# Linear attention and a mixture of experts on one core: the first layer's results in four one-bank tiles, routing's products moved to another bank, and another order of the first loads

## The chip, the core and the metric

The kernel runs on one core of a Trainium2 chip. A core has TensorE (PE, matrix products and transposes; its weight loads are shown as PEld), VectorE (DVE), ScalarE (ACT), GpSimd (POOL), SyncE (SP, which here issues most DMAs) and 16 DMA engines. Products land in PSUM, eight banks of 128 partitions x 512 fp32 values. The metric is the device time of one execution in microseconds.

## The reference

Two steps, all in fp32. First linear attention with positive random features on 8 batches x 8 heads x 576 positions x 64 values (128 features):

```python
def phi(x):                              # x = q or k, scaled by D ** -0.25
    h = einsum('bhsd,md->bhsm', x, omega) - sum(x * x) / 2
    return exp(h - max(h)) / sqrt(m)
kv  = einsum('bhsm,bhsd->bhmd', k_p, v)
z   = sum(k_p, axis=2)
out = einsum('bhsm,bhmd->bhsd', q_p, kv) / (einsum('bhsm,bhm->bhs', q_p, z) + 1e-06)
```

Its result, turned to 4608 rows of 512 values, goes through a mixture of 8 experts. `x @ w_gate` gives each row its expert (the largest logit) and a weight (that expert's softmax). The row's output is the weight times `relu(x @ w1[e]) @ w2[e]`, with w1 512 x 1024 and w2 1024 x 512.

## The kernel before, in words

The order of work on every engine is written out by hand: each engine runs its instructions in the order of the program text, and a framework adds the semaphore waits from what each tile's accesses need. A tile is taken from a pool under a tag; tiles of one tag share that tag's buffers.

**PSUM.** One pool holds all eight banks: tags `tr`, `t2`, `kf` and `nu` of one bank each, and `pp` with two buffers of two banks each.

**Attention** (line 57 on) works in 72 units: for each batch the remainder (head "-1", the last 64 positions of all heads), then its 8 heads. `run` (line 259) is a software pipeline. In iteration i TensorE does, in this order, for unit u = i: the projections (`unit_b1`, L139, into `pp`); for unit i+1 the transposes of k and q (`unit_a1`, L124, into `tr`); for unit i-1 the transposes of q's features (`unit_ct`, L194, into `t2`); for i-2 the gated key-value product (`unit_df`, L211, into `kf`); for i-1 the key-value product (`unit_ckv`, L179, into `kf`); for i-3 the numerators (`unit_dn`, L230, into `nu`). VectorE takes the maximum (L145), copies the transposes (L130) and scales the numerators (L244, L247, which read `nu`). ScalarE does the exponentials (L153) and copies (L187, L199, L217). POOL adds keys (L165 to L167).

**Routing** (line 331 on) puts each row in its expert's list. Its small steps stand in a queue, filled once per batch; `some(n)` runs the next n. It is called twice per iteration: behind `unit_cq`, and behind `unit_dn`. Four steps have TensorE products in a bank of their own tag `kf`: `s0` (L435, in odd batches), `s3` (L456 to L459), and `f0` (L529) and `f5` (L557) of a part that finds the first expert's rows ahead of time. That bank is also the key-value product's.

**Experts** (line 656 on). Rows are gathered in slots of 2 x 128 rows of one expert. `step` (line 844) does for slot t and for four groups g: 24 products of the first layer (`l1`, L788; fp32 as high and low parts, three products each) into bank `p_1[g]`; ScalarE's relu (L802) that reads it and gives the high part hh; VectorE's L806 that reads it and gives the low part hl. Then come the next slot's transposes (L769), and the second layer (`l2`, L813 to L815) into `p_2[0]` and `p_2[1]`, which take the tags `kf` and `nu`. At a change of expert the new weights are split into high and low parts on ScalarE (L51) and VectorE (L45).

The four banks `p_1` are made by `half`, two at a time:

```python
t = self.ps.tile([P, 2, 512], F32, name=f"p_1{len(self.p_1)}", tag="pp", bufs=2)
self.p_1 += [t[:, i, :] for i in range(2)]
```

**The drain of attention.** After the last unit, `run` finishes the last units between the first slot's transposes (`rows`, L697) and the first products of an early slot 0 (`products0`, L714, in plain fp32). The last two units' numerators go to the two banks of one more `pp` tile, `nu_last`; the last remainder's go to `t2`.

**The loads.** `load(b)` (line 93) issues on SP the remainders of k, q and v (`kqr`, and `rv` for v, L105), then k, q and v for two heads at a time (L108). `rv` waits for POOL to clear its tile (L90). The gate weights, which go into tile `G` (L85; L211 reads it), are issued in the constructor, ahead of the first load.

Of the kernel before, what the change touches and what calls it, by code (L numbers as in the profile page):

```python
# [8 lines left out]
F32 = mybir.dt.float32  # L9
# [9 lines left out]
P = 128  # L19
# [4 lines left out]
SM = 512  # L24
# [32 lines left out]
class Attention:  # L57
    def __init__(self, tc, ctx, ps, io, q, k, v, omega, wg, xs, routing, ident):
        self.tc, self.nc = tc, tc.nc
        self.q, self.k, self.v, self.xs, self.routing, self.ident = q, k, v, xs, routing, ident  # L60
        nc = tc.nc
        pool = lambda n, b, **kw: ctx.enter_context(tc.tile_pool(name=n, bufs=b, **kw))
        self.cp = pool("at_c", 1)
        self.io, self.ps = io, ps
        self.wk = pool("at_wk", 2)
        self.xo = pool("at_x", 2)
        cp = self.cp

        om = self.wk.tile([P, 2, D], F32, name="om", tag="kp")
        for i in range(2):  # L70
            nc.sync.dma_start(om[:, i, :], omega)
        pt = self.ps.tile([P, 512], F32, name="pt_om", tag="tr")
        nc.tensor.transpose(pt[:, :P], om.rearrange("p a d -> p (a d)"), ident)
        self.om = cp.tile([P, M], F32, name="omt")
        nc.scalar.mul(self.om, pt[:, :P], SCALE)

        self.G = cp.tile([P, H, W - 1], F32, name="G")
        self.one = cp.tile([P, 1], F32, name="one")
        nc.gpsimd.memset(self.one, 1.0)
        for a in range(2):  # L80
            r = slice(a * D, (a + 1) * D)
            for h in range(H):
                nc.gpsimd.tensor_copy(self.G[r, h, :D], ident[r, r])
            with nc.allow_non_contiguous_dma(reason="gate weights"):
                nc.sync.dma_start(self.G[r, :, D:], wg.rearrange("(h d) e -> d h e", d=D))  # L85


        self.rv = [[cp.tile([P, NP, D], F32, name=f"rv{i}{a}") for a in range(2)] for i in range(2)]
        for t in self.rv[0] + self.rv[1]:
            nc.gpsimd.memset(t, 0.0)  # L90
        self.st, self.last = {}, {}

    def load(self, b):
        nc, io = self.nc, self.io
        s = {}
        s["kqr"] = io.tile([P, 2, NP, D], F32, name=f"kqr_{b}", tag="kqr")
        for nm in "kq":
            s[nm] = io.tile([P, H, NJ, D], F32, name=f"{nm}_{b}", tag=nm)
        s["v"] = io.tile([P, H, NJ, D], F32, name=f"v_{b}", tag="v")
        s["vr"] = self.rv[b % 2]  # L100
        for n, src in enumerate((self.k, self.q, self.v)):
            rem = src[b, :, SM:, :].rearrange("(i a) p d -> a p i d", a=2)
            for a in range(2):
                to = s["vr"][a] if n == 2 else s["kqr"][:, n]
                nc.sync.dma_start(to[a * SR:(a + 1) * SR], rem[a])  # L105
        for c in range(0, H, 2):
            for to, src in ((s["k"], self.k), (s["q"], self.q), (s["v"], self.v)):
                nc.sync.dma_start(to[:, c:c + 2],  # L108
                                  src[b, c:c + 2, :SM, :].rearrange("h (p j) d -> p h j d", j=NJ))
        s["kva"] = self.xo.tile([P, H, W], F32, name=f"kva_{b}", tag="kva")  # L110
        s["x"] = self.xo.tile([P, NJ, H, D], F32, name=f"x_{b}", tag="x")
        s["xr"] = self.xo.tile([P, NP, D], F32, name=f"xr_{b}", tag="xr")
        s["lg"] = self.xo.tile([P, NJ, E, H], F32, name=f"lg_{b}", tag="lg")
        s["lgr"] = self.xo.tile([P, E, NP], F32, name=f"lgr_{b}", tag="lgr")
        self.st[b] = s
# [16 lines left out]
    def unit_b1(self, b, h):  # L132

        nc, s = self.nc, self.st[b]
        t, o = s[("th", h)], self.ps.tile([P, 2, 4, M], F32, name=f"pp_{b}_{h}", tag="pp", bufs=2)
        for n in range(4):
            for a in range(2):
                r = slice(a * D, (a + 1) * D)
                nc.tensor.matmul(o[:, a, n, :], t[r, n, :], self.om[r], start=True, stop=True)  # L139
        s[("pp", h)] = o  # L140
# [78 lines left out]
    def unit_dn(self, b, h):  # L219
        nc, s = self.nc, self.st[b]  # L220
        qt, kva = s[("qt", h)], s["kva"]
        pn = self.last.get((b, h))
        if pn is None:
            pn = self.ps.tile([P, 512], F32, name=f"nu_{b}_{h}", tag="nu")
        o = pn[:, :NJ * W].rearrange("p (j w) -> p j w", w=W)

        for j in range(NJ):
            for a in range(2):
                r = slice(a * SR, (a + 1) * SR)
                nc.tensor.matmul(o[r, j, :], qt[:, j, r], kva[:, h if h >= 0 else 2 * j + a, :], start=True, stop=True)  # L230
        de = self.wk.tile([P, NJ, 1], F32, name=f"de_{b}_{h}", tag="de")
        nc.vector.tensor_scalar_add(de, o[:, :, W - 1:W], EPS)
        s[("nu", h)] = o, de
# [25 lines left out]
    def run(self, pre):  # L259
        units = [(b, h) for b in range(B) for h in [-1] + list(range(H))]  # L260
        n = len(units)
        g = lambda i: units[i] if 0 <= i < n else None
        self.load(0)
        self.unit_a1(*units[0])
        self.unit_a2(*units[0])
        for i in range(n):
            u1, u, c, d, e = g(i + 1), g(i), g(i - 1), g(i - 2), g(i - 3)
            if u[1] == 0 and u[0] + 1 < B:
                self.load(u[0] + 1)
            pre.ahead(i - n)  # L270
            self.unit_b1(*u)
            self.unit_max(*u)
            self.unit_exp(*u, 0)
            if u1: self.unit_a1(*u1)
            else: pre.rows(0)
            if u1: self.unit_a2(*u1)
            self.unit_exp(*u, 1)
            if c: self.unit_ct(*c)
            if c: self.unit_cq(*c)
            self.routing.some(1)  # L280
            self.bank(i)
            if d: self.unit_df(*d)
            if c: self.unit_ckv(*c)
            if d: self.unit_dk(*d)
            if c: self.unit_ckt(*c)
            o = e if e and e[1] >= 0 else (e[0] - 1, -1) if e and e[0] > 0 else None
            if o: self.unit_dn(*o)
            if o: self.unit_rc(*o)
            self.routing.some(2 if i >= n - 6 else 1)
            if o: self.unit_out(*o)  # L290
            self.unit_sum(*u)
        c, d, e = g(n - 1), g(n - 2), g(n - 3)
        self.routing.some(1000)
        self.bank(n)
        two = self.ps.tile([P, 2, 512], F32, name="nu_last", tag="pp", bufs=2)
        self.last = {d: two[:, 0, :], c: two[:, 1, :]}
        self.unit_df(*d)
        self.unit_dk(*d)
        self.unit_dn(*e)
        self.unit_rc(*e)  # L300
        self.unit_out(*e)
        self.unit_ct(*c)
        self.unit_cq(*c)
        pre.rows(1)
        self.unit_ckv(*c)
        self.unit_ckt(*c)
        self.unit_dn(*d)
        self.unit_rc(*d)
        self.unit_out(*d)
        self.unit_df(*c)  # L310
        self.unit_dk(*c)
        pre.banks()
        pre.fill(1)
        self.last[(B - 1, -1)] = self.ps.tile([P, 512], F32, name="nu_rest", tag="t2")
        for o in (c, (B - 1, -1)):
            self.unit_dn(*o)
            self.unit_rc(*o)
            self.unit_out(*o)
# [11 lines left out]

class Routing:


    def __init__(self, tc, ctx, xs, ident):
        self.tc, self.nc, self.xs = tc, tc.nc, xs
# [76 lines left out]
        self.lr[o] = lr  # L412
        self.queue += self.group(b, g, slice(o * NJ, (o + 1) * NJ + o), [self.lr[0], self.lr[1]] if o else None)

    def some(self, n):
        for f in self.queue[:n]:
            f()
        self.queue = self.queue[n:]

    def group(self, b, g, sl, lr):  # L420
        nc, wk = self.nc, self.wk
# [234 lines left out]
class Experts:  # L656
# [40 lines left out]
        self.nc.scalar.copy(self.x0[:, :, a * P:(a + 1) * P], p.rearrange("p (c t) -> p c t", t=P))  # L697

    def banks(self):
        self.p_1 = []  # L700
        self.todo = [m for f in range(self.NF) for m in self.products0(f)]

    def half(self):

        t = self.ps.tile([P, 2, 512], F32, name=f"p_1{len(self.p_1)}", tag="pp", bufs=2)
        self.p_1 += [t[:, i, :] for i in range(2)]

    def products0(self, f):

        def product(c):  # L710
            if c == f % 4 == 0:
                self.half()
            o = self.p_1[f // 2][:, f % 2 * self.T2:(f % 2 + 1) * self.T2]
            self.nc.tensor.matmul(o, self.w1s[:, c, f * P:(f + 1) * P], self.x0[:, c, :],  # L714
                                  start=c == 0, stop=c == self.NC - 1)
# [192 lines left out]
def attention_moe(tc, q, k, v, omega, wg, w1, w2, out, xs):  # L908
    nc = tc.nc
    with ExitStack() as ctx:  # L910
# [7 lines left out]
        with ExitStack() as c2:  # L918
            io = c2.enter_context(tc.tile_pool(name="at_io", bufs=2))
            at = Attention(tc, c2, ps, io, q, k, v, omega, wg, xs, rt, ident)  # L920
            rt.open(ps, "kf")
            with sched():
                at.run(ex)
                ex.rest()
# [26 lines left out]
```

## Time and profile before

| | |
|---|---|
| median of 3 runs | 886.38 us (884.7 to 887.65) |
| the profiled execution | 891.42 us, its span 889.6 us |
| PE busy | 770.4 us (87%) |
| PEld busy | 672.9 us (76%) |
| DVE busy | 364.4 us (41%) |
| ACT busy | 342.6 us (39%) |
| POOL busy | 208.4 us (23%) |
| HBM | 61.10 MB read, 19.55 MB written |

The start takes up to about 16 us of the span, attention with its routing up to about 312 us, the drain and the early slot up to 360 us, the experts the rest. A row of the timeline reads: start in us, length in us, engine, line, operation, out<-in, shape, count, and in brackets how long the engine had been idle before it and what ended that. A row of waits reads: engine, line, what it waited for, us in total, times, longest. Busy times of TensorE are modelled at their ends, so a busy TensorE can still have room.

### The profile page before, as it was taken

The numbers are of one execution on the slowest core, as the hardware profiler recorded it, in microseconds if no ns is written. First come the engines' busy times: TensorE is split into PE (matmuls) and PEld (weight loads), VectorE is DVE, ScalarE is ACT, GpSimd is POOL, SyncE is SP. The second block draws the span as 40 slices with busy tenths as digits, with TensorE's granted clock in tenths as the row PEclk, the third lists the DMA queues.
The fourth block names the chain that finished last, engine by engine and source line by source line (L and its number), as shares of the span: only waits on it lengthen the run. The fifth ranks groups of instructions, "written<-read, shape, count | busy, mean of one in ns | idle before, by whom it ended". The sixth has DMA issues, their size and how long they took to land.

```text
span 889.6 us, 18594 instructions
## 1 busy us (share of the span) xinstructions
PE 770.4 (87%) x7147; PEld 672.9 (76%) x7147; DVE 364.4 (41%) x903; ACT 342.6 (39%) x1016; POOL 208.4 (23%) x364
## 2 busy tenths in 40 slices
PE   5998899988888889889898889888979887989883
PEld 3887788877777776778787778777868776878773
DVE  3677787877867758301111141110151124111110
ACT  2776766766656644311111241111151133111210
POOL 4432433323233311211101120111120111110110
PEclk9999999999989999999999989999989998999997
DMA  5661634606381111521001152101142116100000
GB/s 170 168 202 24 194 87 131 215 5 211 94 300 39 56 56 54 183 97 49 25 29 37 48 166 76 44 30 48 49 141 80 37 48 220 49 29 22 13 25 16
DMA packets 68459, 79.37 MB, mean 89 GB/s; under 512 B 27390, under 2 KB 51966, under 8 KB 68352
## 3 DMA queue, kind: packets, MB, share of 16 engines
q1 hardware_dynamic: 61792, 58.98, 21.1%
q0 software_dynamic: 6560, 19.03, 6.4%
q8 instruction: 59, 0.97, 0.5%
q14 instruction: 48, 0.39, 0.1%
HBM read 61.10 MB, written 19.55 MB: 91 GB/s over the span
## 4 chain that ended last, share of the span: by engine, by line
issue 47%; PE 19%; DVE 10%; DMA 9%; ACT 7%; POOL 5%; POOLq 1%; SPq 0%; DVEq 0%; ACTq 0%
DMA out_dram<-ys,idx 9%; PE pp L139 5%; DVE mx L145 4%; PE kf L179 3%; ACT kp L153 3%; PE nu L230 2%; PE t L194 2%; ACT qp L153 2%; PE tr L124 2%; PE kf L211 2%; POOL xgm L762 1%; POOL xg L762 1%; DVE rt_RH L506 1%; POOL out_dram L821 1%; DVE th L130 1%
## 5 line engine op out<-in xcount | busy, mean ns | idle before, releaser
L788 PE MATMUL p<-xh,w1p 128*128 128x256 f32 x1216 | 177.9, 289 | 65.2 <-DVE hl L806 64.9
L788 PEld LDWEIGHTS p<-xh,w1p 128*128 128x128 f32 x1216 | 160.3, 194 | 75.8 <-DVE hl L806 72.7
L806 DVE SCALAR_TENSOR_TENSOR hl<-p,hh 128x512 fp32r<-128x512 f32 x76 | 52.6, 692 | 387.3 <-ACT hh L802 383.5
L821 POOL DMA_INDIRECT out_dram<-ys,idx x38 | 39.0, 1026 | 430.7 <-ACT ys L820 323.4
L802 ACT ACTIVATE hh<-p 128x512 fp32r<-128x512 f32 x76 | 45.4, 598 | 229.8 <-PE p L788 227.0
L813 PE MATMUL p<-w2p,hh 128*128 128x512 f32 x288 | 115.2, 400 | 0.1
L815 PE MATMUL p<-w2p,hl 128*128 128x512 f32 x288 | 113.6, 394 | 0.0
L814 PE MATMUL p<-w2p,hh 128*128 128x512 f32 x288 | 113.5, 394 | 0.0
L153 ACT ACTIVATE kp<-pp,mx 128x128 f32<-128x128 f32 x256 | 73.2, 368 | 87.7 <-DVE mx L145 87.0
L788 PE MATMUL p<-xl,w1p 128*128 128x256 f32 x608 | 98.2, 284 | 0.0
L820 ACT ACTIVATE ys<-p,gt 128x512 f32<-128x512 f32 x38 | 26.2, 689 | 175.4 <-PE p L815 86.0
L165 POOL TENSOR_TENSOR k<-kp 128x256 f32<-128x256 f32 x64 | 46.5, 726 | 189.5 <-ACT kp L153 140.4
L145 DVE TENSOR_REDUCE mx<-pp 128x8 f32<-128x1024 f32 x64 | 78.1, 1220 | 16.4 <-PE pp L139 11.3
L788 PEld LDWEIGHTS p<-xl,w1p 128*128 128x128 f32 x608 | 84.4, 192 | 0.0
L139 PE MATMUL pp<-omt,th 64*128 64x128 f32 x1024 | 79.1, 297 | 2.1 <-DVE th L130 1.9
L153 ACT ACTIVATE qp<-pp,mx 128x128 f32<-128x128 f32 x256 | 74.3, 398 | 0.0
L139 PEld LDWEIGHTS pp<-omt,th 64*128 64x128 f32 x1024 | 66.4, 198 | 9.8 <-DVE th L130 3.3
L815 PEld LDWEIGHTS p<-w2p,hl 128*128 128x128 f32 x288 | 53.9, 187 | 13.4
L813 PEld LDWEIGHTS p<-w2p,hh 128*128 128x128 f32 x288 | 53.9, 187 | 12.7 <-issue 0.3
L814 PEld LDWEIGHTS p<-w2p,hh 128*128 128x128 f32 x288 | 54.0, 187 | 12.4
L230 PE MATMUL nu<-kva,qt 128*64 128x73 f32 x992 | 55.4, 238 | 0.0
L194 PE MATMUL t<-ident,qp 128*128 128x128 f32 x256 | 42.7, 292 | 4.4 <-ACT qt L199 1.2
(362 smaller groups left out, 1063.1 us busy)
## 6 DMA issues: line engine op xcount, KB each, us to landing
w1s<-in_moe_w_dram SPq DMA_DIRECT2D x5, 2048.0 KB, 9.4
w2s<-in_moe_w_dram SPq DMA_DIRECT2D x5, 2048.0 KB, 10.6
k<-in_k_dram SPq DMA_DIRECT2D x32, 256.0 KB, 5.3
q<-in_q_dram SPq DMA_DIRECT2D x32, 256.0 KB, 5.5
v<-in_v_dram SPq DMA_DIRECT2D x32, 256.0 KB, 5.7
token_rows<-x SPq DMA_DIRECT2D x8, 1024.0 KB, 7.9
kqr<-in_k_dram SPq DMA_DIRECT2D x16, 64.0 KB, 2.9
kqr<-in_q_dram SPq DMA_DIRECT2D x16, 64.0 KB, 2.5
```

What stands on the lines that cost most here:

```text
L139: nc.tensor.matmul(o[:, a, n, :], t[r, n, :], self.om[r], start=True, stop=True)
L145: self.nc.vector.tensor_reduce(out=mx, in_=s[("pp", h)], axis=AX.X, op=ALU.max, negate=True)
L153: self.nc.scalar.activation(o[:, j, :], p[:, a, 2 * n + i, :], AF.Exp, bias=mx[:, a, 2 * n + i:2 * n + i + 1])
L165: nc.gpsimd.tensor_tensor(out=k2, in0=kp[:, :2, :], in1=kp[:, 2:, :], op=ALU.add)
L194: nc.tensor.transpose(pt[:, j * P:(j + 1) * P], qp[:, j, :], self.ident)
L230: nc.tensor.matmul(o[r, j, :], qt[:, j, r], kva[:, h if h >= 0 else 2 * j + a, :], start=True, stop=True)
L788: return [lambda w=w, x=x, c=c, n=n: self.nc.tensor.matmul(o, w[:, c, f], x[:, c, :], start=n == 0, stop=n == len(ops) - 1) for n, (w, x, ...
L806: self.nc.vector.scalar_tensor_tensor(out=b, in0=self.p_1[g], scalar=0.0, in1=a.bitcast(F32), op0=ALU.max, op1=ALU.subtract)
L813: nc.tensor.matmul(p, h[:, c, k], self.w2h[:, c, :], start=c == 0, stop=False)
L814: nc.tensor.matmul(p, h[:, c, k], self.w2l[:, c, :], start=False, stop=False)
L815: nc.tensor.matmul(p, l[:, c, k], self.w2h[:, c, :], start=False, stop=c == self.NF - 1)
L821: self.nc.gpsimd.indirect_dma_start(out=self.out[:, :], in_=y, in_offset=None, bounds_check=NT - 1, out_offset=bass.IndirectOffsetOnAxis(a ...
```

## The change

1. `pp` leaves the common pool: attention has a pool `ps_a` of its own for it (two buffers of two banks). In the drain, behind the last `unit_cq`, that pool is closed, and a pool `ps_m` is opened with four tiles of one bank. `p_1[g]` is tile g of it. The last two units' numerators use tiles 2 and 3 before.
2. Routing's products use tag `nu` instead of `kf`. The first `some` of an iteration stands behind the copy of the transposes, ahead of q's exponentials; the second never runs a step that has products (`PRODUCTS`, by name) and stops ahead of one.
3. The first batch's loads: the remainders of k and q, then k and q of head 0, of head 1, v of both, then v's remainder, then the other heads as before. The gate weights come behind the whole first load. For later batches the order of the loads is as it was.
4. The numerators' products of a unit run their two halves in the order (1, 0).

```diff
@@ Attention.__init__
+        self.open = ExitStack()
+        self.pp = self.open.enter_context(tc.tile_pool(name="ps_a", bufs=2, space=PSUM))
...
-            with nc.allow_non_contiguous_dma(reason="gate weights"):
-                nc.sync.dma_start(self.G[r, :, D:], wg.rearrange("(h d) e -> d h e", d=D))
+        self.wg = wg
@@ Attention.load
-        for n, src in enumerate((self.k, self.q, self.v)):
-            rem = src[b, :, SM:, :].rearrange("(i a) p d -> a p i d", a=2)
-            for a in range(2):
-                to = s["vr"][a] if n == 2 else s["kqr"][:, n]
-                nc.sync.dma_start(to[a * SR:(a + 1) * SR], rem[a])
-        for c in range(0, H, 2):
-            for to, src in ((s["k"], self.k), (s["q"], self.q), (s["v"], self.v)):
-                nc.sync.dma_start(to[:, c:c + 2],
-                                  src[b, c:c + 2, :SM, :].rearrange("h (p j) d -> p h j d", j=NJ))
+        def rest(nms):
+            for n, src in nms:
+                rem = src[b, :, SM:, :].rearrange("(i a) p d -> a p i d", a=2)
+                for a in range(2):
+                    to = s["vr"][a] if n == 2 else s["kqr"][:, n]
+                    nc.sync.dma_start(to[a * SR:(a + 1) * SR], rem[a])
+
+        def main(nms, h):
+            for nm, src in nms:
+                nc.sync.dma_start(s[nm][:, h], src[b, h, :SM, :].rearrange("h (p j) d -> p h j d", j=NJ))
+
+        kq, v = (("k", self.k), ("q", self.q)), (("v", self.v),)
+        rest(((0, self.k), (1, self.q)))
+        if b == 0:
+            main(kq, slice(0, 1))
+            main(kq, slice(1, 2))
+            main(v, slice(0, 2))
+        rest(((2, self.v),))
+        for c in range(2 if b == 0 else 0, H, 2):
+            main(kq + v, slice(c, c + 2))
@@ Attention.unit_b1
-        t, o = s[("th", h)], self.ps.tile([P, 2, 4, M], F32, name=f"pp_{b}_{h}", tag="pp", bufs=2)
+        t, o = s[("th", h)], self.pp.tile([P, 2, 4, M], F32, name=f"pp_{b}_{h}", tag="pp")
@@ Attention.unit_dn
-            for a in range(2):
+            for a in (1, 0):
@@ Attention.run
         self.load(0)
+        for a in range(2):
+            with self.nc.allow_non_contiguous_dma(reason="gate weights"):
+                self.nc.sync.dma_start(self.G[a * D:(a + 1) * D, :, D:], self.wg.rearrange("(h d) e -> d h e", d=D))
...
             if u1: self.unit_a2(*u1)
+            self.routing.some(1)
             self.unit_exp(*u, 1)
             if c: self.unit_ct(*c)
             if c: self.unit_cq(*c)
-            self.routing.some(1)
...
-            self.routing.some(2 if i >= n - 6 else 1)
+            self.routing.some(2 if i >= n - 6 else 1, False)
...
-        two = self.ps.tile([P, 2, 512], F32, name="nu_last", tag="pp", bufs=2)
-        self.last = {d: two[:, 0, :], c: two[:, 1, :]}
...
         self.unit_cq(*c)
+        self.open.close()
+        pre.banks()
+        self.last = {d: pre.bank(2), c: pre.bank(3)}
         pre.rows(1)
...
-        pre.banks()
         pre.fill(1)
@@ Routing
+    PRODUCTS = ("s0", "s3", "f0", "f5")
...
-    def some(self, n):
-        for f in self.queue[:n]:
-            f()
-        self.queue = self.queue[n:]
+    def some(self, n, products=True):
+        while n and self.queue and (products or self.queue[0].__name__ not in self.PRODUCTS):
+            self.queue.pop(0)()
+            n -= 1
@@ Experts
     def banks(self):
+        self.pm = self.ctx.enter_context(self.tc.tile_pool(name="ps_m", bufs=1, space=PSUM))
...
-    def half(self):
-        t = self.ps.tile([P, 2, 512], F32, name=f"p_1{len(self.p_1)}", tag="pp", bufs=2)
-        self.p_1 += [t[:, i, :] for i in range(2)]
+    def bank(self, g):
+        return self.pm.tile([P, 512], F32, name=f"p_1{g}", tag=f"p_1{g}")
...
-            if c == f % 4 == 0:
-                self.half()
+            if c == f % 2 == 0:
+                self.p_1.append(self.bank(f // 2))
@@ attention_moe
-            rt.open(ps, "kf")
+            rt.open(ps, "nu")
```

## The prediction

> **What bounds the kernel now.** I read the page first, then the busy times by stage, then TensorE's waits, then the order of time at the places that those waits name.
>
> ```profile
> span 889.6 us, 18594 instructions
> ```
> ```profile
> 50.00:312.00 262.00, 237.09 (x3476) 207.35 (x3474) 199.85 (x573) 176.66 (x657) 91.13 (x164) 0.95 0.43 132
> ...
> 360.00:870.00 510.00, 444.64 (x2808) 397.05 (x2807) 107.94 (x168) 116.19 (x203) 85.33 (x111) 0.98 0.19 64
> ```
>
> The columns of the stage rows are length, PE, PEld, DVE, ACT, POOL, granted clock, DMA share, GB/s. TensorE is the engine that is full: 237 of 262 us in attention, 445 of 510 in the experts, where VectorE and ScalarE are busy a fifth of the time. What matters is why TensorE stops, and where its clock is halved. In the experts its idle time has one name, L806, the hidden layer's low part:
>
> ```profile
> PEld p L788 <- DVE hl L806: 72.7, 38, 4.8
> PE p L788 <- DVE hl L806: 64.9, 38, 4.6
> ```
> ```profile
> 390.04 0.60 ACT L802 ACTIVATE hh<-p 128x512 fp32r<-128x512 f32 x1 [2.06 <-PE p L788]
> 390.67 0.69 DVE L806 SCALAR_TENSOR_TENSOR hl<-p,hh 128x512 fp32r<-128x512 f32 x1 [13.08 <-ACT hh L802]
> ...
> 391.41 1.21 PE L788 MATMUL p<-xh,w1p 128*128 128x256 f32 x8 [1.47 <-DVE hl L806]
> ...
> 394.23 1.01 PEld L788 LDWEIGHTS p<-xh,w1p 128*128 128x128 f32 x8
> ...
> 398.74 1.01 PEld L788 LDWEIGHTS p<-xh,w1p 128*128 128x128 f32 x8 [1.62 <-DVE hl L806]
> ```
>
> A step has four groups g of 24 products. Group 1 starts at 391.41, after waiting for group 0's L806; group 2 at 394.23 without a wait; group 3 at 398.74, after waiting for group 2's. L806 reads p_1[g], the next group writes p_1[g+1]. Only 0-1 and 2-3 wait, and these are the pairs that share one two-bank tile. The wait follows the tile, not the bank. Two other places agree:
>
> ```profile
> 324.96 0.41 DVE L247 TENSOR_TENSOR x<-nu_last,de 128x256 f32<-128x256 f32 x1
> ...
> 325.52 0.73 PE L230 MATMUL nu_last<-kva,qt 128*64 128x73 f32 x16 [0.19 <-DVE x L247]
> ```
> ```profile
> 381.61 0.69 ACT L820 ACTIVATE ys<-p,gt 128x512 f32<-128x512 f32 x1 [4.97 <-PE p L815]
> ...
> 381.82 0.39 PE L815 MATMUL p<-w2p,hl 128*128 128x512 f32 x1
> ...
> 386.72 0.40 PE L815 MATMUL p<-w2p,hl 128*128 128x512 f32 x1
> ```
>
> nu_last is the other two-bank tile: products into its second bank wait for a read of its first. p_2's banks are one-bank tiles, and L815 runs on in one while L820 reads the other.
>
> **The change part by part.**
>
> *Four one-bank tiles for p_1.* Each group then writes a tile whose readers ran a step earlier. A group without a wait takes 394.23 less 391.41 = 2.82 us; from group 2 to group 3 it is 398.74 less 394.23 = 4.51, so a usual wait costs 1.69, and three long ones more. The weight-load row sums them to 72.7; I take 73, between the matmul row's 65 (whose ends are modelled) and 75. Late next is nothing: the second layer needs group 3's L806 only in its 21st product, and 21 products take 386.72 less 381.82 = 4.9 us, while L802 and L806 take 0.60 + 0.69.
>
> *The clock in the experts.* The three long waits (4.3 us and more) come at a change of expert, where L802 stands behind eight casts of weights on ScalarE. The group behind such a wait runs at half clock:
>
> ```profile
> 522.34 4.26 ACT L51 CAST w2p<-w2s 128x512 fp32r<-128x512 f32 x8
> ```
> ```profile
> 528.56:533.84 5.28, 5.28 (x24) 5.28 (x25) 0.50 0.89 241
> 558.18:561.00 2.82, 2.82 (x24) 2.82 (x25) 1.00 0.59 183
> ```
>
> The same 24 products take 5.28 against 2.82, 2.5 us more. Three times that is 7, which I take. Below it lies 0 (the clock drops anyway), above it 510 x (1 - 0.98) = 10.
>
> *Routing's products in the nu bank, behind the transposes.* Now they use kf, behind the copy L187 or ahead of L211:
>
> ```profile
> PE rr L456 <- ACT kvt L187: 11.3, 5, 2.5
> PE kf L211 <- DVE m L463: 3.0, 2, 2.0
> PE h_cnt L529 <- ACT kvt L187: 1.9, 1, 1.9
> PE rf L435 <- ACT kvt L187: 1.9, 1, 1.9
> PE kf L211 <- DVE rt_L L436: 1.4, 2, 0.7
> ```
> ```profile
> 112.13 0.18 PE L456 MATMUL rr<-rt_OH,rt_tri 128*128 128x40 bf16 x1 [2.10 <-ACT kvt L187]
> ...
> 112.35 1.16 PE L139 MATMUL pp<-omt,th 64*128 64x128 f32 x16
> ```
>
> Together 19.5 us (us in total, times, longest). At 112.13 the next unit's projection, L139, is queued behind the waiting product, so the whole unit slips. In the new order the product stands behind L139 and the transposes (1.16 us and more after the numerators), and nu's last reader, L247, belongs to the unit before; kf is left alone. The new wait is that of the next numerators for routing's read of nu, with the unit's transposes and key-value products between: I allow 0.1 to 0.2 us for each of 12 groups of products, 2 in all. The products' own time stays; a routing step comes half a unit later at most, and what uses the result (the gather of the first rows) stands whole units behind. So 17.5, from 8 (half the waits come back) to 19.5.
>
> Behind these stalls too the clock is halved; the first and the last of seven such stretches:
>
> ```profile
> 70.90:74.20 3.30, 3.30 (x28) 2.74 (x28) 2.22 (x5) 0.63 (x3) 0.00 (x0) 0.54 0.00 0
> ...
> 303.00:306.30 3.30, 3.30 (x38) 3.08 (x34) 1.27 (x8) 1.62 (x7) 1.36 (x3) 0.54 0.02 5
> ```
>
> Attention's 0.95 over 262 us is 13 us of full speed lost. I take 10 of it back, from 0 to 13. [...] The trace speaks for 10: each halved stretch stands behind a routing stall.
>
> *The halves of the numerators, (1, 0).* With the remainder's key-value product ahead, and without it (a unit behind a remainder):
>
> ```profile
> 93.26 0.27 PE L179 MATMUL kf<-kp_-1_1424,rv 128*64 128x128 f32 x1
> ...
> 94.08 1.16 PE L139 MATMUL pp<-omt,th 64*128 64x128 f32 x16
> ```
> ```profile
> 241.75 0.71 PE L230 MATMUL nu<-kva,qt 128*64 128x73 f32 x16
> ...
> 242.52 1.16 PE L139 MATMUL pp<-omt,th 64*128 64x128 f32 x16
> ```
>
> 0.82 against 0.77: that product, which fills the first half, costs 0.05 now. If the second half's numerators run beside it, up to 64 x 0.05 = 3 is won; if not, 0. I take 1.
>
> *k and q first.* Rows of the start:
>
> ```profile
> 1.75 1.42 SPq L85 DMA_DIRECT2D G<-in_moe_w_gate_dram  x2
> ...
> 3.21 1.29 SPq L105 DMA_DIRECT2D kqr<-in_k_dram  x2
> ...
> 9.03 1.29 SPq L105 DMA_DIRECT2D rv<-in_v_dram  x2
> ...
> 10.37 0.60 SPq L108 DMA_DIRECT2D k<-in_k_dram  x1
> ...
> 11.31 1.23 DVE L145 TENSOR_REDUCE mx_-1_228<-pp_-1_219 128x8 f32<-128x1024 f32 x1 [2.18 <-PE pp_-1_219 L139]
> ...
> 13.64 0.66 PE L124 MATMUL tr<-ident,k 128*128 128x128 f32 x2 [2.38 <-DMA k<-in_k_dram]
> ...
> 15.77 2.08 PE L139 MATMUL pp<-omt,th 64*128 64x128 f32 x16 [0.78 <-DVE th L130]
> ```
> ```profile
> 25.59 0.35 PE L211 MATMUL kf<-G,kvt 128*64 128x72 f32 x4
> ```
>
> SP's queue holds head 0's k behind rv, which waits until 9.03 for POOL to clear its tile. Without G ahead, kqr goes out at 1.75, 1.46 earlier, and so the first maximum starts at 9.85. Head 0's k goes out near 4.4 and lands 13.64 - 10.37 = 3.3 later, at 7.7, before TensorE is free of the first projection. Its transposes then end near 11.2, their copy waits for the maximum's end at 11.1, and L139 follows at 11.95 instead of 15.77: 3.8 gained. G goes out behind the nine remaining loads (up to 0.60 us each from 10.4, so near 15.8, and takes 1.42 to issue), and L211 would want it at 25.59 - 3.8 = 21.8. With 3.3 us to land it is there at 20.5; in a fuller queue it may be late, and then L211 and all behind it wait. I take 3.5, from 1 to 4.5. For later batches the order of the loads stays as it is.
>
> *The drain.* The new pool's tiles stand on the old pp slots, whose last readers are the exponentials of the last unit; TensorE has by then passed the transposes of their results. So nothing waits that did not wait, and nu_last's 0.19 goes: 0, from -1 to 1.
>
> Sum: 73 + 7 + 17.5 + 10 + 1 + 3.5 = 112. The profiled execution took 891.4 (span 889.6 and 1.8 around it) and would take 779; the median of the runs, 886.4, is 5.0 lower, which gives **774**.
>
> **The rivals.**
>
> *The wait stays.* The tiles of one pool might be watched together, or the wait have another owner. Then only 32 us come, and the median would be 854. [...] For it: the wait is there in spite of four banks. Against it: no wait between groups 1 and 2, none in p_2.
>
> *The long waits move.* At a change of expert the second layer waits for casts and L806 instead of the first. Three waits of 4.8 and their 7 us of slow clock come back, 21: 795. Against it: casts have the 11.3 us of four unbroken groups to finish.
>
> *Routing's stalls return in nu.* 27.5 are lost: 802 (774 + 27.5). For it: VectorE is busy 200 of 262 us there, and every unit's numerators use this one bank.
>
> *Slower.* TensorE without pauses is granted less clock, through attention and experts. After the change they last about 262 - 27.5 and 510 - 80, 665 us at full clock; a clock c adds 665 x (1/c - 1), and the 112 are eaten at c = 0.86. At 0.80 the time would be 774 + 166 = 940. Against it: the longest unbroken stretches, from one step's second layer into the next, show 1.00.
>
> **How the numbers follow.** The forecast's own case gets 0.79, the moved long waits 0.06, the returned routing stalls 0.05, the wait that stays 0.06, the slower clock 0.02, and 0.02 is left for no change. Low: all upper bounds, 75 + 10 + 19.5 + 13 + 3 + 4.5 + 1 = 126, so 760. High: the lower bounds 65 + 0 + 8 + 0 + 0 + 1 - 1 = 73 would give 813, but not all fall together; 797 holds the moved waits, and leaves out the last three cases and most of the routing one. Range 760 to 797. No change means within 0.3% (2.7 us), which is what the three runs spread. Faster 0.96, same 0.02, slower 0.02.
>
> **What would show it.** A step is now 418.22 less 391.41, 26.8 us:
>
> ```profile
> 418.22 1.21 PE L788 MATMUL p<-xh,w1p 128*128 128x256 f32 x8 [1.47 <-DVE hl L806]
> ```
>
> Right: L806 gone from TensorE's waits, a step of 23.4 us (26.8 less two waits), 1.00 in the experts; no L456 or L435 behind L187, and near 1.00 in attention; the second L139 near 12 us and L211 at 22 with no DMA ahead of it. Wrong: L788 still behind L806; L813 to L815 with a wait ahead of them; L230 behind L463 or L436; a granted clock below 1.00 in long stretches.

## Result and the profile after

| | before | after |
|---|---|---|
| median of 4 runs each | 886.09 us (884.7 to 887.65) | 778.29 us (777.73 to 778.81) |
| ratio | | 0.8783 (0.8767 to 0.8799) |
| the profiled execution, and its span | 891.42, 889.6 | 777.73, 775.9 |
| PE busy | 770.4 us (87%) | 740.8 us (95%) |

The kernel is 107.8 us faster by the medians, 113.7 by the two profiled executions. The prediction said 774, with a range of 760 to 797. Lines of the changed kernel are numbered higher: attention by 12 (L139 is L151, L187 is L199, L211 is L223, L230 is L242, L247 is L259), routing and the experts by 16 (L456 is L472, L788 is L804, L806 is L822, L815 is L831).

The busy times by stage of the changed kernel: attention, drain, experts.

```profile
span 775.9 us, 18503 instructions
```
```profile
50.00:285.00 235.00, 225.13 (x3449) 194.84 (x3447) 201.24 (x572) 174.55 (x653) 90.85 (x164) 1.00 0.46 144
285.00:332.00 47.00, 43.20 (x356) 31.33 (x355) 30.02 (x110) 20.11 (x51) 9.00 (x16) 1.00 0.27 88
332.00:760.00 428.00, 427.55 (x2805) 387.31 (x2804) 106.84 (x167) 114.81 (x201) 85.61 (x112) 1.00 0.22 77
```

The third column is TensorE's busy time. In the experts it is 427.55 of 428 us, and the granted clock is 1.00 in all three stages, from 50 to 760 us. TensorE's waits in the changed kernel, and the group of the first layer's products, whose last figure is the idle time ahead of it:

```profile
PE t L206 <- ACT qt L211: 4.6, 17, 0.4
...
PE kf L223 <- ACT kvt L199: 2.3, 1, 2.3
PE rr L472 <- DVE x L259: 1.5, 2, 0.8
...
PE nu L242 <- DVE h_v L547: 0.9, 1, 0.9
```
```profile
L804 PE MATMUL p<-xh,w1p 128*128 128x256 f32 x1216 | 167.8, 280 | 0.3
```

The 38 waits for the low part are gone (0.3 us of idle time is left), and so are routing's waits behind the copy L199. What remains behind the start is 1.1 us at most at a time, but for one wait of 2.3 us in the drain (L223 behind L199), which the kernel before had too. One kind of wait has grown: that of the transposes of q's features (L206) for ScalarE's copy of those before them. A step of the experts by the timeline, first products of two steps running:

```profile
376.56 1.10 PE L804 MATMUL p<-xh,w1p 128*128 128x256 f32 x8
...
399.95 1.10 PE L804 MATMUL p<-xh,w1p 128*128 128x256 f32 x8
```

It is 23.39 us, where it was 26.81. The start, in the same view:

```profile
1.76 1.40 SPq L107 DMA_DIRECT2D kqr<-in_k_dram  x2
...
4.51 0.60 SPq L111 DMA_DIRECT2D k<-in_k_dram  x1
...
10.08 1.23 DVE L157 TENSOR_REDUCE mx_-1_233<-pp_-1_224 128x8 f32<-128x1024 f32 x1 [2.18 <-PE pp_-1_224 L151]
...
11.96 2.08 PE L151 MATMUL pp<-omt,th 64*128 64x128 f32 x16 [0.88 <-DVE th L142]
...
22.56 0.35 PE L223 MATMUL kf<-G,kvt 128*64 128x72 f32 x4
```

Head 0's projection starts at 11.96 instead of 15.77 and waits for no DMA ahead of it. L223 starts at 22.56 without waiting for the gate weights.

Where the 113.7 us lie, between the same instructions in both profiled executions:

| stretch | before | after | difference | forecast |
|---|---|---|---|---|
| to the maximum of batch 1's remainder | 46.8 | 43.4 | -3.4 | -3.5 |
| from there to the maximum of the last head | 267.9 | 242.8 | -25.1 | -28.5 |
| from there to the first L788 (L804): the drain | 45.1 | 43.2 | -1.9 | 0 |
| from there to the end of the last L815 (L831) | 515.9 | 432.8 | -83.2 | -80 |

### The profile page after: what moved, and what is told of

Read it like the earlier page. It is cut to its first block, busy times and chain, and to the rows that moved or that the text cites. A ratio compares the mean times of both kernels' runs of the same rounds, so it can differ in the third digit from the quotient of the medians.

```text
span 775.9 us, 18503 instructions
## 1 busy us (share of the span) xinstructions
PE 740.8 (95%) x7147; PEld 650.9 (84%) x7147; DVE 366.7 (47%) x903; ACT 341.4 (44%) x1016; POOL 208.6 (27%) x364
## 5 line engine op out<-in xcount | busy, mean ns | idle before, releaser
L822 DVE SCALAR_TENSOR_TENSOR hl<-p,hh 128x512 fp32r<-128x512 f32 x76 | 52.2, 690 | 304.5 <-ACT hh L818 302.3
L804 PE MATMUL p<-xh,w1p 128*128 128x256 f32 x1216 | 167.8, 280 | 0.3
L804 PEld LDWEIGHTS p<-xh,w1p 128*128 128x128 f32 x1216 | 154.5, 188 | 3.1 <-issue 1.6
L829 PE MATMUL p<-w2p,hh 128*128 128x512 f32 x288 | 115.2, 400 | 0.1
L831 PE MATMUL p<-w2p,hl 128*128 128x512 f32 x288 | 113.6, 394 | 0.0
L818 ACT ACTIVATE hh<-p 128x512 fp32r<-128x512 f32 x76 | 45.1, 597 | 147.3 <-PE p L804 145.1
L804 PE MATMUL p<-xl,w1p 128*128 128x256 f32 x608 | 95.9, 279 | 0.0
L177 POOL TENSOR_TENSOR k<-kp 128x256 f32<-128x256 f32 x64 | 46.8, 732 | 160.8 <-ACT kp L165 128.6
L804 PEld LDWEIGHTS p<-xl,w1p 128*128 128x128 f32 x608 | 82.0, 188 | 0.0
L151 PE MATMUL pp<-omt,th 64*128 64x128 f32 x1024 | 76.0, 289 | 1.9 <-DVE th L142 1.5
L151 PEld LDWEIGHTS pp<-omt,th 64*128 64x128 f32 x1024 | 63.6, 191 | 8.5 <-DVE th L142 4.2
L831 PEld LDWEIGHTS p<-w2p,hl 128*128 128x128 f32 x288 | 53.9, 187 | 13.3
L829 PEld LDWEIGHTS p<-w2p,hh 128*128 128x128 f32 x288 | 54.0, 187 | 12.7 <-issue 0.3
L242 PE MATMUL nu<-kva,qt 128*64 128x73 f32 x992 | 53.0, 229 | 0.9 <-DVE h_v L547 0.9
L242 PEld LDWEIGHTS nu<-kva,qt 128*64 128x64 f32 x992 | 49.0, 136 | 1.5 <-DVE h_v L547 1.0
```

Source lines behind the costliest of these rows:

```text
L177: nc.gpsimd.tensor_tensor(out=k2, in0=kp[:, :2, :], in1=kp[:, 2:, :], op=ALU.add)
L804: return [lambda w=w, x=x, c=c, n=n: self.nc.tensor.matmul(o, w[:, c, f], x[:, c, :], start=n == 0, stop=n == len(ops) - 1) for n, (w, x, ...
L818: self.nc.scalar.activation(a, self.p_1[g], AF.Relu)
L822: self.nc.vector.scalar_tensor_tensor(out=b, in0=self.p_1[g], scalar=0.0, in1=a.bitcast(F32), op0=ALU.max, op1=ALU.subtract)
L829: nc.tensor.matmul(p, h[:, c, k], self.w2h[:, c, :], start=c == 0, stop=False)
L831: nc.tensor.matmul(p, l[:, c, k], self.w2h[:, c, :], start=False, stop=c == self.NF - 1)
```

## Experiments

The theory after this result was that of the prediction, with four independent parts: the wait belongs to the shared tile; routing's stalls belong to its place and its bank; the lost clock belongs to both kinds of waits; the loads give the start. The rivals were that another part of the change carried the experts' gain (the pool's opening, the reordered drain), that the parts lean on each other, and that the clock has a cause of its own.

**The tiles alone.** The kernel before with part 1 of the change.

```diff
+        self.pp = self.open.enter_context(tc.tile_pool(name="ps_a", bufs=2, space=PSUM))
...
+        self.pm = self.ctx.enter_context(self.tc.tile_pool(name="ps_m", bufs=1, space=PSUM))
...
+        return self.pm.tile([P, 512], F32, name=f"p_1{g}", tag=f"p_1{g}")
```

> The kernel before with part 1 alone (the pool opened in the drain, four one-bank tiles). Theory, by the tile: the 38 waits of L788 behind L806 and the three halved stretches of the experts go, 80 to 85 us, about 803 us; routing's stalls behind L187 and a granted clock of about 0.95 in attention stay. Rival, by pool or bank: about 886 us. Rival, the parts help each other (the clock is earned back only when all stalls go): clearly less than 80.

Measured: 805.19 us (804.85 to 806.1) beside 886.93 for the kernel before on the same chip; ratio 0.9086 (0.907 to 0.9102), 81.7 us. Its stages, attention and experts, and its longest waits of routing (lines two further on than in the kernel before, so L458 is L456):

```profile
50.00:312.00 262.00, 236.59 (x3514) 206.01 (x3511) 203.34 (x583) 179.34 (x667) 92.12 (x166) 0.97 0.43 132
360.00:780.00 420.00, 419.55 (x2765) 380.84 (x2765) 105.71 (x166) 114.25 (x200) 84.58 (x110) 1.00 0.23 78
```
```profile
PE rr L458 <- ACT kvt L189: 11.3, 5, 2.5
```

The experts are as full as in the whole change. Attention keeps its stalls: the waits are the same 11.3 us, and TensorE is busy 236.6 us of the same 262 (237.1 before). The experts' gain is this part's alone.

**Routing alone.** The kernel before with the new bank and the new places.

```diff
-            rt.open(ps, "kf")
+            rt.open(ps, "nu")
...
+            self.routing.some(1)
             self.unit_exp(*u, 1)
...
-            self.routing.some(1)
...
-            self.routing.some(2 if i >= n - 6 else 1)
+            self.routing.some(2 if i >= n - 6 else 1, False)
```

> The kernel before with part 2 alone (routing's products in nu, behind the transposes). Theory: no L456, L529 or L435 behind L187, attention's clock back to 1.00, 25 us less, about 861 us; the experts unchanged with 38 waits. Rival, the stalls only move to the numerators: less than 10 us.

Measured: 863.41 us (863.16 to 863.74), ratio 0.9744 (0.9726 to 0.9761), 23.5 us. Attention in this kernel, and the experts' wait (one line further on):

```profile
50.00:285.00 235.00, 226.03 (x3463) 195.95 (x3460) 201.15 (x574) 176.81 (x659) 90.96 (x164) 1.00 0.48 147
```
```profile
PE p L789 <- DVE hl L807: 64.9, 38, 4.6
```

Attention's clock is 1.00, and the 38 waits in the experts are untouched.

**The places without the bank.** As the last, with the products still in `kf`.

```diff
             rt.open(ps, "kf")
...
-            self.routing.some(2 if i >= n - 6 else 1)
+            self.routing.some(2 if i >= n - 6 else 1, False)
```

> The kernel before with the new places of routing's steps, but its products still in kf. Theory: with the products behind the transposes L187 of the unit before is done, so the 15 us behind L187 go and with them most of the slow clock, while L211 now waits 0.7 to 2 us for routing's read of kf behind every product (some 10 us): 10 to 18 us less than before, 868 to 876. Rival, the bank is what counts: within 5 us of before. Rival, the order is all: as fast as with the bank, about 861.

Measured: 869.14 us (868.76 to 869.54), ratio 0.9808 (0.9791 to 0.9825), 17.8 us. Routing's product (L457 is L456) and the product behind it:

```profile
PE rr L457 <- ACT kvt L187: 3.4, 7, 0.7
...
PE kf L211 <- DVE m L464: 2.7, 7, 1.1
```
```profile
50.00:293.00 243.00, 227.78 (x3465) 195.62 (x3464) 200.34 (x574) 176.61 (x658) 91.06 (x164) 1.00 0.46 142
```

In the new places the products still wait for the copy in `kf`, but 0.7 us at most instead of 2.5, and L211 behind them 1.1. The clock is already at 1.00. So the places give 17.8, and the bank 5.7 more. The bank without the places was not tried; there the numerators and routing's products might wait for each other in the one bank, which no run shows.

**The loads alone.**

```diff
-        for n, src in enumerate((self.k, self.q, self.v)):
...
+        rest(((0, self.k), (1, self.q)))
+        if b == 0:
+            main(kq, slice(0, 1))
...
```

> The kernel before with the loads' new order alone. Theory: head 0's projection starts near 12 instead of 15.8 us and the gain stays, 3.4 us less, about 882.7 us. Rival: taken back by later waits for loads or gate weights, within 1 us of before.

Measured: 883.05 us (10 runs, 881.42 to 885.08), ratio 0.9962 (0.9943 to 0.998), 3.9 us. Head 0's projection and one new wait for the gate weights (L149 is L139 here, L221 is L211):

```profile
11.88 2.08 PE L149 MATMUL pp<-omt,th 64*128 64x128 f32 x16 [0.88 <-DVE th L140]
```
```profile
PE kf L221 <- DMA G<-in_moe_w_gate_dram: 0.7, 1, 0.7
```

The parts add up: 81.7 + 23.5 + 3.9 = 109.1, against 886.93 - 778.29 = 108.6 for the whole. Within what the runs can tell, nothing is left for the order of the halves, which was not run alone, and the parts do not lean on each other.

**One pool, but shared tiles.** The changed kernel, with `p_1` as two tiles of two banks in the new pool. Pool, drain and order stay as in the change.

```diff
-        return self.pm.tile([P, 512], F32, name=f"p_1{g}", tag=f"p_1{g}")
+        if g % 2 == 0:
+            self.pair = self.pm.tile([P, 2, 512], F32, name=f"p_1{g}", tag=f"p_1{g}")
+        return self.pair[:, g % 2, :]
```

> The changed kernel with one thing undone: p_1 is two two-bank tiles of the new pool again (tiles 0-1 and 2-3). Theory, the wait follows the tile: L788's 38 waits behind the low part are back, with the long ones at three changes of expert and a halved clock behind these, 80 to 85 us more, 858 to 863 us. Rival, it was the new pool or its place: 778 us, no such wait.

Measured: 860.06 us (859.45 to 862.35), 81.8 above the changed kernel; ratio to the kernel before 0.9693 (0.9678 to 0.9708).

```profile
PE p L806 <- DVE hl L824: 64.9, 38, 4.6
```
```profile
332.00:840.00 508.00, 442.65 (x2798) 395.45 (x2797) 107.92 (x168) 115.61 (x203) 85.50 (x111) 0.98 0.19 64
```

The lines are two further on than in the changed kernel: L806 is the first layer's product, L824 the low part. With the same pool and the same 7147 products, all 38 waits and 64.9 us are back. The tile makes the wait, and nothing else in part 1.

**The long waits alone.** The kernel before, with the casts of w2 behind group 0's relu and low part, so that L802 no longer stands behind them at a change of expert.

```diff
-            if t > 1:
-                self.change(t, 2)
...
             self.hlow(t, g)
+            if g == 0 and t > 1:
+                self.change(t, 2)
```

> The kernel before with the eight casts of w2 at a change of expert moved behind group 0's relu and low part. The 38 waits stay, but the three long ones become as short as the others (1.5 instead of 4.3 to 4.6 us): 9 us. Theory, the halved clock in the experts is the long waits' doing: the granted clock there is 1.00 and 5 to 8 us more go, 14 to 17 in all, about 871 us. Rival, the change of expert itself (its weights' loads and casts) halves the clock: the halved stretches stay and only 9 us go, about 878.

Measured: 870.16 us (869.36 to 872.45), ratio 0.9818 (0.9803 to 0.9833), 17.0 us. The waits, and the experts:

```profile
PE p L788 <- DVE hl L806: 38.1, 26, 1.5
PE p L788 <- DVEq L826: 17.6, 12, 1.5
```
```profile
360.00:850.00 490.00, 435.24 (x2787) 387.88 (x2786) 104.92 (x164) 113.43 (x198) 83.49 (x110) 1.00 0.20 66
```

There are 38 waits still (12 of them put down to VectorE's queue at L826), but none over 1.5 us, and the clock is 1.00. The waits became 64.9 - 38.1 - 17.6 = 9.2 us shorter; the other 7.8 of the 17.0 are clock. The halved clock in the experts came from the three long waits, as forecast (7), not from the 35 short ones.

**A version beyond: start and drain.** In the changed kernel the first loads wait in SP's queue, and one stall is left in the drain:

```profile
287.97 0.76 PE L242 MATMUL nu<-kva,qt 128*64 128x73 f32 x14
291.02 0.35 PE L223 MATMUL kf<-G,kvt 128*64 128x72 f32 x4 [2.30 <-ACT kvt L199]
```

This kernel issues omega, q's first remainder and the gate weights from ScalarE, and puts the transposes of the last unit's features ahead of that L223.

```diff
-            nc.sync.dma_start(om[:, i, :], omega)
+            nc.scalar.dma_start(om[:, i, :], omega)
...
+        rest(((0, self.k),))
+        rest(((1, self.q),), nc.scalar.dma_start if b == 0 else nc.sync.dma_start)
...
+        self.unit_ct(*c)
+        self.unit_cq(*c)
         self.unit_df(*d)
```

> The changed kernel with omega, the first remainder of q and the gate weights issued from ScalarE's queue beside SP's, and in the drain the last unit's transposes and their copy ahead of the product that waits 2.3 us for L199's copy. Theory: first projection near 6.4 instead of 7.95 us, 1.5 us there, and about 1 us in the drain: 775.8. Rival: the start is bound behind it by the loads or POOL, and the copy on ScalarE delays the drain as much as it fills: 778.

Measured: 776.91 us (775.95 to 779.71), ratio to before 0.8762 (0.8746 to 0.8778). The first projection starts at 8.11, not at 6.4. The drain's stall is not gone, it has another name: the transposes wait for ScalarE's copy of the transposes before them, which stands behind exponentials on ScalarE until 288.92:

```profile
289.62 0.65 PE L207 MATMUL t<-ident,qp 128*128 128x128 f32 x4 [2.01 <-ACT qt L212]
```

**Its start alone.** The same, with the drain as in the change.

```diff
-            nc.sync.dma_start(om[:, i, :], omega)
+            nc.scalar.dma_start(om[:, i, :], omega)
...
+        rest(((1, self.q),), nc.scalar.dma_start if b == 0 else nc.sync.dma_start)
```

> The changed kernel with the start's part of that alone (omega, the first remainder of q and the gate weights from ScalarE's queue). Theory: 1.5 us less, 776.8. Rival: 778, taken back by the third unit's loads or by the exponentials behind ScalarE's issues.

Measured: 776.56 us (775.6 to 778.08), ratio 0.8756 (0.8744 to 0.8767). The first projection starts at 8.12:

```profile
2.46 0.74 ACTq L107 DMA_DIRECT2D kqr<-in_q_dram  x1
...
3.93 0.45 PE L75 MATMUL pt_om<-ident,om 128*128 128x128 f32 x1 [3.93 <-DMA om<-in_omega_dram]
...
4.60 1.28 ACT L77 ACT_TABLE_LOAD   x1 [4.60 <-DMA om<-in_omega_dram]
...
6.22 1.11 PE L137 MATMUL tr_-1_217<-ident,kqr 128*128 128x128 f32 x4 [1.84 <-ACT omt L77]
```

Here lies the miss: omega is used at 3.93 instead of 3.34, and ScalarE, busy with issuing until 4.6, loads its table only then (at 0.82 in the changed kernel). The copy of omega comes behind it, and the transposes wait for that copy. What q gained, omega lost.

**q's remainder alone from ScalarE.** Omega and the gate weights stay on SP.

```diff
-        rest(((0, self.k), (1, self.q)))
+        rest(((0, self.k),))
+        rest(((1, self.q),), nc.scalar.dma_start if b == 0 else nc.sync.dma_start)
```

> The changed kernel with the first remainder of q alone issued from ScalarE's queue, omega and the rest from SP's. Theory: q's transposes follow k's at once, the first projection starts near 7.3 instead of 7.95 us, 0.7 us less than the changed kernel, at the edge of what the runs can tell. Rival: no difference, or later, if ScalarE's queue delivers later, as it did for omega (3.9 instead of 3.3 us).

Measured: 777.78 us (775.42 to 779.2), ratio 0.8772 (0.875 to 0.8793). The first projection starts 0.68 earlier than the changed kernel's 7.95:

```profile
7.27 2.08 PE L152 MATMUL pp_-1_224<-omt,th_-1_222 64*128 64x128 f32 x16 [0.78 <-DVE th_-1_222 L143]
```

Its time and the changed kernel's 778.25 on the same chip (below) overlap. These three versions end up to 1.7 us below the changed kernel's 778.29; whether any of them is faster is not settled.

**The same kernels again.** Three kernels without an edit: the kernel before, twice, and the changed kernel, for the spread and the clock of single executions.

> The kernel before once more, one profiled execution. The profiled execution that the forecast was worked out on took 891.4 us and held seven halved stretches of 3.4 us in attention, one in the drain and three of 6.8 us in the experts, a mean clock of 0.967. Theory: its 5 us over the median are clock, since a stall is followed by a half-speed stretch in some executions and not in others, and by 3.4 or 6.8 us; an execution near 886 has a mean clock of 0.971 to 0.975 (0.006 of 886 us are 5.3), one near 890 has 0.967. Rival: the time and the clock do not go together.

> The same kernel again, a second execution for the same question: time and mean clock go together, 1 us for each 0.0011 of clock. Rival: they do not.

> The changed kernel again beside the next one. Theory: 778 us, the runs within 1.5 us of each other, since no stall is left that the clock falls behind; before spread over some 6 us. Rival: as wide as before.

Measured: before 886.16 and 887.05 us, one execution each; the changed kernel 778.25 us (776.37 to 778.67), ratio 0.8774 (0.8755 to 0.8792). Span and mean clock of the two new executions of the kernel before, and of the one that the prediction reads:

```profile
core 0: 884.5 us, clock 0.974
```
```profile
core 0: 885.3 us, clock 0.973
```
```profile
core 0: 889.6 us, clock 0.967
```

Span times clock is an estimate of the time at full speed: 861.5, 861.4 and 860.2 us. They agree to 1.3 us, while the spans differ by 5.1. The 31 other executions of the kernel before that ran beside these experiments bear it out: their spans lie between 882.1 and 888.3 us, span and clock go together (correlation -0.92), and the product lies between 859.0 and 862.3. The execution of the prediction lost 889.6 - 860.2 = 29.4 us to the clock, the other two 23.0 and 23.9. Some 5 to 6 us of that are the end, where TensorE has no work. The rest, summed over windows of 0.85 us as length times one less the clock, is in attention, drain and experts 11.9, 1.7 and 10.2 us in the execution of the prediction (23.8), 8.5, 1.7 and 6.8 in the one at 886.16 (17.0), and 6.8, 1.7 and 10.2 in the other (18.7). The changed kernel's 2.3 us of spread in five runs is more than the 1.5 expected, and about half of the kernel before's in nine on the same chip (884.2 to 888.72).

## Why the prediction was right, and where it missed

*Four tiles and the experts' clock: 80 forecast, 81.7 alone, 83.2 between the two profiles.* The reading that carried it was that only groups 0-1 and 2-3 waited. The kernel with pairs shows it. The step is 23.39 us where 23.4 was worked out, so the price of 1.69 for a wait was right. Of the 83.2 some 73 are waits and 10.2 are clock. The 7 for the clock was too small for that execution: it was priced on one group of 5.28 us, and each of the three halved stretches lasts 6.8 us.

*Routing: 17.5 of waits and 10 of clock forecast, 23.5 measured alone.* The direction of both is shown: the places take the stalls of 2 us away and with them the halved clock, the bank takes the rest. The size was too large. Attention between the same instructions (the table's second stretch), before and after:

```profile
46.80:314.70 267.90, 242.81 (x3561) 212.29 (x3560) 204.95 (x587) 181.47 (x676) 92.63 (x168) 0.96 0.42 129
```
```profile
43.40:286.20 242.80, 232.79 (x3561) 201.33 (x3559) 207.78 (x587) 180.79 (x676) 92.68 (x168) 1.00 0.46 143
```

TensorE's idle time fell from 25.1 to 10.0, by 15.1 us; its busy time for the same products fell by 10.0, which is clock. Routing's own waits went about as forecast, from 20.1 to 2.4 us; the 2.4 are the 1.5 and 0.9 behind `nu`, where 2 was allowed. But the transposes of q's features wait more for ScalarE's copy of those before them: 3.4 us in all before (L194 behind L199), 6.2 after (L206 behind L211), and 6.4 in the kernel with routing alone. The prediction has no term for this wait; why that copy comes later was not taken apart. The clock's 10 fits the execution that it was read from. In the two executions taken later TensorE was busy 239.7 and 238.1 us in this stretch, only 6.9 and 5.3 more than after the change, so for a median the 10 was too large.

One reading of the prediction does not hold: that each halved stretch stands behind a routing stall. Six of the seven in attention stand behind waits of 1.9 to 2.5 us; ahead of the one at 254.8 TensorE waited 0.6 us at most.

*Halves of the numerators: 1 forecast, 0 measured.* The median from the remainder's key-value product to the next projection is 0.82 us before and after, so the new order won nothing there.

*Loads: 3.5 forecast, 3.9 alone, 3.4 between the profiles.* The second projection came at 11.96, where 11.95 was worked out.

*Drain: 0 forecast, 1.9 measured.* No new wait came. The kernel before lost 1.7 us to the clock there, in a halved stretch behind its stall of 2.3 us; the changed kernel's profile has the stall and no halved stretch. That is most of the 1.9, and it depends on the execution: the last section shows one of a later version in which the clock falls there.

*The step that failed* is attention's part of the sum, 17.5 + 10 + 1 = 28.5. From the execution at the median (886.16 us) to the changed kernel's profile the four stretches of the table give 3.9, 21.3, 1.9 and 81.6 us, 108.7 together, where 3.5, 28.5, 0 and 80 were forecast. Attention is 7.2 short. In that execution TensorE's idle time there was 24.4 us, which gives 14.4 instead of 17.5, for the most part because of the waits of L206 that the prediction did not have; its busy time gives 6.9 instead of 10; the halves give nothing instead of 1. The other stretches gave 3.9 more than forecast. That the time came out only 4 us beside the forecast is thus in part luck.

*The last line of the sum*, "the median of the runs, 886.4, is 5.0 lower, which gives 774", is not where the 4 us went. The 5.0 was lost clock, and it was not counted twice: the terms 7 and 10 take back 17 of the 23.8 us that the profiled execution lost. After the change only the drain's stall is left to lose clock behind, and the profiled execution (777.73) stands 0.6 below it, not 5 above. That the sum's 779 for the profiled execution came near those 777.73 is luck again: between the profiles attention gave 3.4 less than forecast, experts and drain 3.2 and 1.9 more.

*The rivals.* The wait that stays is refuted by the tiles alone; its price, 854, is near what the kernel with pairs shows (860). Long waits that move: L829 to L831 have 0.1 us of idle time in all. Stalls that return in `nu`: 2.4 us. A slower clock for a TensorE without pauses: 1.00 over 428 us at 427.55 busy.

## What to carry to other kernels

A tile that spans several PSUM banks is one thing to the framework's waits (38 waits and 64.9 us with pairs in the new pool, 0.3 us of idle time with tiles of one bank): give every group that is written and read apart a tile of its own, and find such pairs by asking which of several equal groups wait. Work that has no hurry goes on an in-order engine behind what is sure to be ready, not ahead of it, in a buffer whose readers are long done (17.8 us for the places here, 5.7 more for the bank). Before a saving is taken off a median, ask what the profiled execution has more than the median one (here 5 us of lost clock), and which terms were read from it.

## What the runs showed of the hardware

*The same wait halves the clock in one execution and not in another.* The two later executions of the kernel before, each with the same stall of 2.16 us ahead of routing's product, and the stretch behind it:

```profile
70.21 0.18 PE L456 MATMUL rr<-rt_OH,rt_tri 128*128 128x32 bf16 x1 [2.16 <-ACT kvt L187]
```
```profile
70.90:74.30 3.40, 3.40 (x30) 2.85 (x26) 2.38 (x7) 0.64 (x3) 0.00 (x0) 0.52 0.00 0
```
```profile
70.55 0.18 PE L456 MATMUL rr<-rt_OH,rt_tri 128*128 128x32 bf16 x1 [2.16 <-ACT kvt L187]
```
```profile
70.55:73.95 3.40, 3.40 (x54) 3.09 (x55) 2.71 (x7) 0.60 (x3) 0.08 (x1) 1.00 0.00 0
```

30 products in 3.4 us in the first, 54 in the second. The last column but two is the clock, 0.52 and 1.00. Behind the 38 waits of 1.5 us at most in the kernel with late casts the experts stay at 1.00; behind waits of 1.9 to 2.5 us it happens in some executions.

*The halved stretches begin whole multiples of one length apart.* In the profiled execution that the prediction reads, those in which TensorE has work begin at 70.50, 145.59, 186.56, 220.69, 254.82, 265.06, 302.61, 319.68, 527.89, 661.01 and 742.93 us. The first eight last 3.41 us each, the last three 6.83. The starts are whole multiples of 3.413 us apart, to within 0.01 us; the length is fitted to these eleven. The first stretch, with the same length ahead of it:

```profile
67.09:70.50 3.41, 0.94 (x23) 0.86 (x22) 1.34 (x7) 2.91 (x11) 1.62 (x3) 1.00 0.00 0
70.50:73.91 3.41, 3.41 (x24) 2.90 (x22) 2.33 (x6) 0.34 (x2) 0.00 (x0) 0.50 0.00 0
```

In attention of the two later executions the clock of windows of 3.4 us puts the starts at 70.7, 145.8, 186.8, 220.9 and 261.9 us in the first, and at 144.8, 185.7, 219.8 and 254.0 in the second. Within each they fit the same length to within 0.1 us. Cut into windows of that length from these starts, the stall above looks so in the first execution, and so in the second:

```profile
67.34:70.75 3.41, 1.25 (x29) 1.17 (x28) 1.31 (x8) 2.82 (x11) 1.62 (x3) 1.00 0.02 5
```
```profile
66.29:69.70 3.41, 2.10 (x40) 1.88 (x39) 2.50 (x8) 2.25 (x10) 1.02 (x3) 1.00 0.02 5
69.70:73.12 3.42, 2.57 (x37) 2.26 (x38) 1.90 (x5) 0.80 (x4) 0.85 (x2) 1.00 0.00 0
```

In the first it lies inside one window and leaves TensorE 1.25 us of work in it; in the second a boundary cuts it in two, and 2.10 and 2.57 us are left. That the place of the stall picks the execution is a reading of these rows; no run moved a stall to show it. In the execution of the prediction, cut in the same way, the clock fell eleven times from 44 us on and as long as TensorE had work. In the window before, TensorE had been busy 0.43 of the time or less nine times, and 0.55 and 0.73 the other two, which stay open. The emptiest window there that was followed by full clock had 0.56. In the experts a halved stretch began in none of the 35 waits of about 1.5 us, which leave 1.9 of 3.41, and in each of the three long ones (4.34, 4.63 and 4.57 us). In the changed kernel's profile, cut from the start of the half clock at its end (764.96 us), the drain's stall leaves 0.48 of one window, and full clock follows.

The changed kernel's one long stall, in the drain, does the same. In the kernel with q's remainder from ScalarE the clock behind it is halved, in the changed kernel's profile it is not:

```profile
288.90 0.34 PE L224 MATMUL kf<-G,kvt 128*64 128x72 f32 x4 [2.29 <-ACT kvt L200]
```
```profile
289.60:293.00 3.40, 3.40 (x31) 2.92 (x30) 0.86 (x4) 1.17 (x2) 0.00 (x0) 0.53 0.00 0
```
```profile
291.00:294.40 3.40, 3.38 (x62) 3.09 (x64) 0.86 (x4) 1.56 (x4) 0.00 (x0) 1.00 0.00 0
```

A stretch of 3.4 us at 0.53 costs 1.6 us, which is of the size of the spread that is left to the changed kernel; that it makes this spread was not shown, for only some executions have a trace.
